# Head-by-head key and query loads with 32 partitions outermost, a later value load, and new durations in a hand-written plan: sketched linear attention and a ReGLU block on Trainium2

## The chip, the cores and the metric

One Trainium2 chip, one core. The metric is the device time of one launch in microseconds (us), the median over runs. All times below are us from the start of the profiled span unless a unit is given. PE is TensorE (matmul), DVE VectorE, ACT ScalarE, POOL GpSimd, SP SyncE; SP, ACT and POOL also issue the transfers (DMAs).

## What is computed

Four batches b, four heads h, 1088 positions, head size 32, sketch rank 8, then a feed-forward block over 4352 tokens of width 128 with 1536 hidden columns:

```
phi(x) = outer(S1 x, S2 x) flattened           # 64 features per position
kv = sum_s phi(k) v^T ;  z = sum_s phi(k)      # per batch and head
attn = (phi(q) kv) / (phi(q) z + 1e-6)
x = attn as [4352, 128]                        # heads side by side
out = (relu(x w_gate) * (x w_val)) w_out
```

q, k, v, the sketches, the weights and the output are float32; the wide matmuls run in float16.

## The kernel before

**Stages.** For each batch a key object K(b) loads the keys, transposes them on DVE (`t1`, or `t1q` for batch 0, and `t1r` for the last 64 positions), sketches them on PE (L330), transposes back (`t2`, L350), sums z on PE (`zsum`, L364), masks it on DVE (`zevac`, L370), multiplies it out on PE (`w`, L377) and writes it into the query weights on ACT (`wevac`, L382); POOL (DVE for one part of batch 0) makes the outer products (`phi`, L249), and PE accumulates kv with the values (L389). The values of batch 0 are loaded as float32 into `v32` and cast on ACT (L307); the others are cast by their DMA. Nine query groups Q(g) (the first with 8 columns of 32 positions per head, the others with 16, so that a group can reach over a batch's edge) go through DVE transpose (L459), sketch on PE (L468), transpose back on DVE (L475), denominator (POOL L485, DVE L489 and L493), outer products (POOL L497, L249), PE transpose (L509), ACT copy (L513), PE product with kv (L521) and ACT copy into `xT` (L528). The feed-forward block is cut into 51 pairs, 3 for group 0 and 6 for each other group: gate and value matmuls (L553), relu on ACT (L566), product on DVE (L570), output matmuls (L579), and at the end of a group a scaled copy on ACT (L585) and stores on SP (L605).

**Order.** Each engine runs its instructions strictly in the order in which they were written. The start is written out by hand: loads of batch 0 on SP and ACT (L164 to L174), then constants, the weight loads on POOL, and 48 idle matmuls on zeros (L222) that keep PE busy before its first real work (L225, L230). Everything after goes into `Plan`, a list scheduler in Python (L21 to L76): each operation is added with an engine, a duration, dependencies, a due time and an earliest time `at`; `Plan.run` simulates the engines and picks by latest start. Only the order comes out of it: nothing waits for a planned time on the chip. The inputs of the plan are the durations in the `P.add` calls, the landing times of the loads (`land`, `qland`, L533 to L538), the time of the first pair `T0` and the step between pairs `PACE` (L255, L256), and the time from which each engine is free (L649). Where the planned gap on PE before the first pair is long, L655 fills in more matmuls on zeros.

**Loads.** Keys go in four blocks of 256 positions for a batch, each for all four heads (L138); the last 64 positions in a load of their own (L143); queries in one load per batch (for batch 0 in two, columns 0 to 8 first, L172 and L174). In `load_k` the outermost dimension of the source is the head:

```
eng.dma_start(out=kA[b][:, blk], in_=k[b, :, 256*blk:256*blk+256, :].rearrange("h (t q) d -> h t (q d)", q=8))
```

The built program gives the loads and stores of SP and ACT together eight completion semaphores in rotation: from the ninth on, each issue waits on its queue until the load issued eight places before has landed. SP issues in this order: S2, blocks 0 and 2 of batch 0, its rest (`load_kr`), the first queries, the rest of the values, the other queries of batch 0, and then for each of the batches 1 to 3 four blocks, the rest and the queries: 25 loads, ahead of the stores. ACT issues S1, blocks 1 and 3, and the values of batch 0, and then loads its function table (L179).

Of the kernel before, what the change touches and what calls it, by code (L numbers as in the profile page):

```python
# [79 lines left out]
def kernel(  # L80
# [12 lines left out]
    nc = tc.nc  # L93

    B, H, S, D = q.shape
    R = S1.shape[0]
# [38 lines left out]
    wv = sb("wv", [DM, NJ, 128], FP16)  # L135
    wo = sb("wo", [128, NJ, DM], FP16)

    def load_k(eng, b, blk):  # L138
        eng.dma_start(out=kA[b][:, blk],
                      in_=k[b, :, 256 * blk:256 * blk + 256, :].rearrange(  # L140
                          "h (t q) d -> h t (q d)", q=8))

    def load_kr(eng, b):  # L143
        eng.dma_start(out=kR[b], in_=k[b, :, 1024:, :].rearrange("h (t e) d -> h t (e d)", e=2))
# [5 lines left out]
    def load_vr(eng, dst, b):  # L150
        eng.dma_start(out=dst[0:64, :, 8, :], in_=v[b, :, 1024:, :].rearrange("h p d -> p h d"))

    def load_q(eng, b, lo, hi):
        eng.dma_start(out=qA[:, b * NT + lo:b * NT + hi, :],
                      in_=q[b].rearrange("h (t n) d -> (h t) n d", n=NT)[:, lo:hi, :])

    def load_w(dst, src, lo, hi):
        nc.gpsimd.dma_start(out=dst[:, lo:hi], in_=src.rearrange("m (j f) -> m j f", f=128)[:, lo:hi])
# [2 lines left out]
        nc.gpsimd.dma_start(  # L161
            out=wo[:, lo:hi], in_=moe_w_out.rearrange("(j f) m -> f j m", f=128)[:, lo:hi])

    nc.scalar.dma_start(out=s16[0:R], in_=S1[:, None, :].to_broadcast([R, 4, D]))  # L164
    nc.sync.dma_start(out=s16[R:2 * R], in_=S2[:, None, :].to_broadcast([R, 4, D]))
    load_k(nc.sync, 0, 0)
    load_k(nc.scalar, 0, 1)
    load_k(nc.sync, 0, 2)
    load_k(nc.scalar, 0, 3)
    load_kr(nc.sync, 0)  # L170
    load_v(nc.scalar, v32, 0)
    load_q(nc.sync, 0, 0, 8)  # L172
    load_vr(nc.sync, v32, 0)
    load_q(nc.sync, 0, 8, NT)  # L174

    zero = sb("zero", [128, 128], FP16)
    nc.vector.memset(zero, 0.0)
    scr = sb("scr", [1, 1], FP16)
    nc.scalar.activation(out=scr, in_=zero[0:1, 0:1], func=ACTF.Relu)  # L179

    id32 = sb("id32", [2 * R, 2 * R])
    make_identity(nc, id32)
# [70 lines left out]
            op=ALU.mult)  # L253

    T0 = 11.5  # L255
    PACE = 1.65  # L256

    class K:


        def __init__(self, b, land, cuts, engs):
            self.b = b
            n, i = f"k{b}", ["DVE", "POOL"]
            self.kT = rot("kT", b, 2, [128, 34, 32])
            self.ab = rot("abk", b, 2, [128, NQ, 2, 2, 2 * R])
            self.kp = rot("kp", b, 2, [128, 2, NQ, 2, R * R], FP16)
            self.zm = rot("zm", b, 2, [128, 4 * R])
            if b == 0:
                t1 = [P.add("DVE", 0.58, lambda x=x: self.t1q(x, x + 4), at=land[0]) for x in (0, 4)]
            else:  # L270
                t1 = [P.add("DVE", 0.6, lambda x=x: self.t1(x, x + 2),
                            [kk[b - 2].kvx] if b > 1 else [], at=land[0]) for x in (0, 2)]
            t1.append(P.add("DVE", 0.14, self.t1r, at=land[-1]))
            ab = []
            for lo, hi in zip(cuts, cuts[1:]):
                ab.append(P.add("PE", 0.09 * (hi - lo), lambda lo=lo, hi=hi: self.sketch(lo, hi),
                                [*t1[:1 if b == 0 and hi == 4 else 3], *ab[-1:]], take=("V", n), lat=0.25))
            t2, ph = [], []
            for lo, hi in zip(cuts, cuts[1:]):
                last = hi == NQ  # L280
                t2.append(P.add("DVE", 0.14 + 0.067 * (hi - lo), lambda lo=lo, hi=hi: self.t2(lo, hi),
                                [ab[len(t2)], *t2[-1:]], give=(n,) if last else ()))
            zs = []
            for lo, hi in zip(cuts, cuts[1:]):
                zs.append(P.add("PE", 0.083 * (hi - lo), lambda lo=lo, hi=hi: self.zsum(lo, hi),
                                [t2[len(zs)], *zs[-1:]], take=("M", n + "m"), lat=0.25))
            self.z = zs[-1]
            zm = P.add("DVE", 0.18, self.zevac, [self.z])
            w = P.add("PE", 0.45, self.w, [zm], lat=0.25)
            self.wst = P.add("ACT", 0.25, self.wevac, [w])  # L290
            kv = []
            for (lo, hi), e in zip(zip(cuts, cuts[1:]), engs):
                for h2 in range(2):
                    eng = e[h2]
                    ph.append(P.add(
                        eng, (0.16 + 0.145 * (hi - lo)) if eng == "DVE" else 0.1 + 0.27 * (hi - lo),
                        lambda h2=h2, lo=lo, hi=hi, eng=eng: self.phi(h2, lo, hi, eng),
                        [t2[cuts.index(lo)]]))
                kv.append(P.add("PE", 0.115 * (hi - lo), lambda lo=lo, hi=hi: self.kv(lo, hi),
                                [self.z, *ph[-2:], *kv[-1:], *self.vdeps(land)], lat=0.25))  # L300
            self.kvx = P.add("DVE", 0.28, self.kvevac, [kv[-1], zm], give=(n + "m",))
# [115 lines left out]
    class Q:  # L417


        def __init__(self, g, land):  # L420
            self.g = g
            n0, nn = self.n0, self.nn = groups[g]
            self.parts = parts(n0, nn)
            bs = [b for b, _, _ in self.parts]
            m = self.m = nn // 2
            self.qT = rot("qT", g, 4, [128, 16, 32])[:, 0:nn]
            self.ab = rot("abq", g, 4, [128, 8, 2, 32])[:, 0:m]
            self.qp = rot("qp", g, 4, [128, 8, 2, R * R], FP16)[:, 0:m]
            self.pt = rot("pt", g, 4, [128, 8, 128], FP16)[:, 0:m]
            self.dn = rot("dn", g, 4, [128, 16])[:, 0:2 * m]  # L430
            self.rd = rot("rd", g, 4, [128, 16])[:, 0:2 * m]
            self.an = rot("an", g, 4, [128, 16, R])[:, 0:2 * m]
            n = f"q{g}"
            f = nn / 16
            need = T0 + PACE * first[g] - 0.2
            old = [qq[g - 4].xx] if g > 3 else []
            t1 = P.add("DVE", 0.06 + 0.52 * f, self.t1, old, at=max(land[b] for b in bs))
            ab = P.add("PE", 0.1 + 0.5 * f, self.sketch, [t1, *(kk[b].wst for b in bs)],
                       take=("V", n), lat=0.25)
            t2 = P.add("DVE", 0.12 + 0.54 * f, self.t2, [ab], give=(n,))  # L440
            e = "DVE" if g == 0 else "POOL"
            d1 = P.add(e, 0.25 if g == 0 else 0.45, lambda: self.bwm(e), [t2])
            d2 = P.add("DVE", 0.15 + 0.15 * f, self.red, [d1])
            d3 = P.add("DVE", 0.2, self.rec, [d2])
            d4 = P.add(e, 0.25 if g == 0 else 0.42, lambda: self.am(e), [d3])
            if g == 0:
                ph = [P.add("DVE", 0.62, lambda: self.phi(0, 3, "DVE"), [d4]),
                      P.add("POOL", 0.42, lambda: self.phi(3, 4, "POOL"), [d4])]
            else:
                ph = [P.add("POOL", 0.08 + 0.235 * 4, lambda lo=lo: self.phi(lo, lo + 4, "POOL"), [d4])  # L450
                      for lo in (0, 4)]
            tr = P.add("PE", 0.47 * f, self.tr, ph, take=("M", n + "t"), lat=0.2)
            te = P.add("ACT", 0.15 + 0.75 * f, self.tre, [tr], give=(n + "t",))
            nu = P.add("PE", 0.2 + 0.25 * f, self.num, [te, *(kk[b].kvx for b in bs)],
                       take=("M", n + "x"), lat=0.25)
            self.xx = P.add("ACT", 0.15 + 0.42 * f, self.x, [nu], give=(n + "x",), due=need - 0.6)

        def t1(self):
            nc.vector.transpose(self.qT.rearrange("p n t -> p (n t)"),  # L459
# [70 lines left out]
                    "p (a t s) -> p a t s", a=4, s=ns),  # L530
                in_=m_ps[:, 0:32 * self.nn].rearrange("p (a s t) -> p a t s", a=4, s=ns))

    kk = [K(0, [4.6, 4.7, 4.9, 5.0, 6.5, 5.2], [0, 4, 9], [("DVE", "POOL"), ("POOL", "POOL")])]  # L533
    qland = [5.5, 14.0, 18.0, 22.0]
    qq = [Q(0, qland)]
    for b in range(1, B):
        kk.append(K(b, [[0, 12.0, 16.0, 20.0][b]] * 2, [0, 5, 9], [("POOL", "POOL")] * 2))
    qland[0] = 8.0  # L538
    for g in range(1, 9):
        qq.append(Q(g, qland))  # L540

# [67 lines left out]
    for i, (g, y) in enumerate(pairs):  # L609
# [3 lines left out]
        for z in range(2):  # L613
            gm.append(P.add("PE", 0.22, lambda i=i, z=z: gate(i, z), [qq[g].xx, lastpe, *gm],
                            due=due + 0.3 * z, take=("G", f"g{i}{z}"), lat=0.2))
            rel.append(P.add("ACT", 0.57, lambda i=i, z=z: relu(i, z),
                             [gm[-1], *(pro[i - 3:i - 2] if i > 2 else [])],
                             due=due + 0.6 + 0.5 * z, give=(f"g{i}{z}",)))
        vm = P.add("PE", 0.435, lambda i=i: val(i), [gm[-1]], due=due + 0.7,
# [12 lines left out]
    for eng, at, fn in [  # L632
# [4 lines left out]
        ("POOL", 9.4, lambda: load_vr(nc.gpsimd, v_sb[1], 1)),  # L637
    ]:
        P.add(eng, 0.6, fn, at=at, due=at + 2.0)
    for b in range(1, B):  # L640
        for blk in range(4):
            P.add("SP", 0.45, lambda b=b, blk=blk: load_k(nc.sync, b, blk), at=5.0, due=4.0 * b)
        P.add("SP", 0.45, lambda b=b: load_kr(nc.sync, b), at=5.0, due=4.0 * b + 0.1)
        P.add("SP", 0.45, lambda b=b: load_q(nc.sync, b, 0, NT), at=5.0, due=4.0 * b + 0.2)
        if b > 1:
            P.add("POOL", 0.8, lambda b=b: load_v(nc.gpsimd, v_sb[b], b), at=6.0 * b, due=8.0 * b)
            P.add("POOL", 0.6, lambda b=b: load_vr(nc.gpsimd, v_sb[b], b), at=6.0 * b, due=8.0 * b)

    order = P.run({"PE": 4.2, "DVE": 4.3, "ACT": 4.2, "POOL": 5.2, "SP": 5.0})  # L649
    pe = 4.2  # L650
    go = qq[0].xx["end"]
    for o in order:
        if o["eng"] == "PE":
# [34 lines left out]
```

## Time and profile before

| what | value |
|---|---|
| runs shown | 136.34, 139.30, 139.46 us, median 139.30 |
| the profiled execution | 136.85 us, of it 135.1 us span |
| PE busy in the span | 112.6 us (83%), 1306 matmuls |
| DVE, ACT, POOL busy | 91.0, 77.0, 51.7 us |
| first transpose of keys (L319) | 13.45 |
| first gate matmul (L553) | 26.28 |
| first product (L570) | 31.22 |
| first gate of group 2, pair 9 of 0 to 50 (L553) | 51.02 |
| last output copy (L585) ends | 128.07 |
| mean granted PE clock | 0.916 |

The page divides the span into 40 slices of 3.38 us. Busy shares and the granted clock are in tenths of each slice. A busy PE is not PE at its peak, since the ends of matmuls are modelled. In the chain of work that ended last each row has a start, a length and the instruction or the transfer that held the end back. In the timeline a row has a start, a length, engine, line, operation, tiles and the count, and in brackets how long the engine had been idle and what ended that.

### The profile page before, as it was taken

The numbers are of one execution on the slowest core, as the hardware profiler recorded it, in microseconds if no ns is written. First come the engines' busy times: TensorE is split into PE (matmuls) and PEld (weight loads), VectorE is DVE, ScalarE is ACT, GpSimd is POOL, SyncE is SP. The second block draws the span as 40 slices with busy tenths as digits, with TensorE's granted clock in tenths as the row PEclk, the third lists the DMA queues.
The fourth block names the chain that finished last, engine by engine and source line by source line (L and its number), as shares of the span: only waits on it lengthen the run. The fifth ranks groups of instructions, "written<-read, shape, count | busy, mean of one in ns | idle before, by whom it ended". The sixth has DMA issues, their size and how long they took to land.

```text
span 135.1 us, 3196 instructions
## 1 busy us (share of the span) xinstructions
PE 112.6 (83%) x1306; PEld 73.5 (54%) x1306; DVE 91.0 (67%) x145; ACT 77.0 (57%) x137; POOL 51.7 (38%) x73
## 2 busy tenths in 40 slices
PE   6930799963989999999999999999999999999500
PEld 6920486842645763747675374766546556546200
DVE  4010678719369989888897885689678799579400
ACT  0400120383255668974876896577599988898300
POOL 7400393992761527109570700946170017000000
PEclk9995555999599999999999999999999999999965
DMA  0699337999635510110020011013002103012011
GB/s 11 146 261 230 82 117 210 156 142 245 104 80 116 180 64 0 22 58 5 13 69 0 2 29 53 0 13 70 0 0 43 39 0 63 17 14 71 0 30 48
DMA packets 10143, 9.47 MB, mean 70 GB/s; under 512 B 3664, under 2 KB 8400, under 8 KB 10128
## 3 DMA queue, kind: packets, MB, share of 16 engines
q1 hardware_dynamic: 4752, 6.46, 17.4%
q0 software_dynamic: 4544, 2.02, 12.3%
q10 hardware_dynamic: 832, 0.79, 1.8%
q8 instruction: 10, 0.16, 0.5%
q14 instruction: 5, 0.04, 0.1%
HBM read 9.05 MB, written 2.23 MB: 83 GB/s over the span
## 4 chain that ended last, share of the span: by engine, by line
PE 51%; DMA 18%; ACT 10%; DVE 4%; issue 4%; POOL 3%; SPq 3%; ACTq 1%; POOLq 1%; DVEq 0%
PE g_ps L553 14%; PE o_ps L579 12%; PE d_ps L553 12%; DMA v<-in_v_dram 10%; DMA kA<-in_k_dram 8%; ACT g_sb L566 4%; ACT pt L513 3%; DVE ht L570 3%; PE m_ps L509 3%; POOL qp L249 2%; PE m_ps L364 2%; PE m_ps L521 2%; PE d_ps L330 2%; PE d_ps L468 2%; ACT xT L528 2%
## 5 line engine op out<-in xcount | busy, mean ns | idle before, releaser
L566 ACT ACTIVATE g_sb<-g_ps 128x512 f16<-128x512 f32 x102 | 56.9, 599 | 19.7 <-PE g_ps L553 18.3
L570 DVE TENSOR_TENSOR ht<-g_sb,d_ps 128x1024 f16<-128x1024 f16 x51 | 61.1, 1209 | 10.1 <-ACT g_sb L566 6.3
L553 PE MATMUL g_ps<-xT,wg 128*128 128x512 f16 (+1 forms) x108 | 35.1, 367 | 1.5 <-ACT g_sb L566 0.3
L579 PEld LDWEIGHTS <-ht 128*128 128x128 f16 x408 | 27.6, 114 | 10.8 <-DVE ht L570 4.0
L579 PE MATMUL o_ps<-wo,ht 128*128 128x128 f16 x408 | 31.8, 221 | 0.7 <-DVE ht L570 0.7
L553 PE MATMUL d_ps<-xT,wv 128*128 128x512 f16 (+1 forms) x108 | 30.8, 372 | 0.0
L249 POOL TENSOR_TENSOR kp<-abk 128x640 f16<-128x640 f32 (+1 forms) x15 | 17.4, 1181 | 28.4 <-DVE abk L350 28.4
L249 POOL TENSOR_TENSOR qp<-an,abq 128x512 f16<-128x512 f32 (+1 forms) x17 | 17.5, 1050 | 3.0 <-DVE an L497 2.4
L553 PEld LDWEIGHTS <-wg 128*128 128x128 f16 x108 | 10.1, 100 | 9.2 <-issue 3.3
L513 ACT COPY pt<-m_ps 128x1024 f16<-128x1024 f16 (+1 forms) x9 | 8.7, 963 | 7.8 <-PE m_ps L509 7.7
L220 PE MATMUL o_ps<-zero 128*128 128x128 f16 x115 | 11.6, 277 | 1.1 <-DVE mask L204 1.1
L485 POOL TENSOR_TENSOR bw<-abq 128x128 f32<-128x128 f32 x8 | 3.6, 456 | 23.0 <-DVE abq L475 23.0
L553 PEld LDWEIGHTS <-wv 128*128 128x128 f16 x108 | 9.2, 98 | 5.9 <-issue 2.6
L330 PE MATMUL d_ps<-kT,skS 64*32 64x160 f32 (+2 forms) x128 | 4.2, 329 | 9.5 <-DVE kT L319 6.4
L220 PEld LDWEIGHTS <-zero 128*128 128x128 f16 x115 | 9.9, 129 | 1.8 <-DVE mask L204 1.1
L475 DVE STREAM_TRANSPOSE abq<-d_ps 128x512 f32<-128x512 f32 (+1 forms) x9 | 6.1, 683 | 2.7 <-PE d_ps L468 2.7
L330 PEld LDWEIGHTS d_ps<-kT,skS 64*32 64x32 f32 x128 | 1.6, 117 | 11.6 <-DVE kT L319 6.6
L311 DVE STREAM_TRANSPOSE kT<-kA 128x512 f32<-128x512 f32 x6 | 4.1, 681 | 5.1 <-DMA kA<-in_k_dram 5.1
L585 ACT ACTIVATE o_sb<-o_ps 128x512 f32<-128x512 f32 (+1 forms) x9 | 5.2, 573 | 2.5 <-PE o_ps L579 2.5
L459 DVE STREAM_TRANSPOSE qT<-qA 128x512 f32<-128x512 f32 (+1 forms) x9 | 5.8, 652 | 1.1 <-DMA qA<-in_q_dram 1.1
L468 PE MATMUL d_ps<-qT,wst 64*64 64x256 f32 (+7 forms) x96 | 6.5, 368 | 0.0
L307 ACT CAST v_sb<-v 128x1152 f16<-128x1152 f32 x1 | 1.2, 1152 | 9.3 <-DMA v<-in_v_dram 9.3
(66 smaller groups left out, 84.0 us busy)
## 6 DMA issues: line engine op xcount, KB each, us to landing
kA<-in_k_dram SPq DMA_DIRECT2D x14, 128.0 KB
qA<-in_q_dram SPq DMA_DIRECT2D x3, 544.0 KB
out_dram<-o_sb SPq DMA_DIRECT2D x5, 256.0 KB
v_sb<-in_v_dram POOLq DMA_DIRECT2D x3, 256.0 KB, 9.2
v<-in_v_dram ACTq DMA_DIRECT2D x1, 512.0 KB
qA<-in_q_dram SPq DMA_DIRECT2D x1, 416.0 KB
out_dram<-o_sb SPq DMA_DIRECT2D x2, 192.0 KB
kA<-in_k_dram ACTq DMA_DIRECT2D x2, 128.0 KB
```

The lines of the kernel that those rows point to most:

```text
L220: nc.tensor.matmul(o_ps[:, 0], zero, zero, start=True, stop=True)
L249: eng.tensor_tensor(out=dst.rearrange("p x (i j) -> p x i j", i=R), in0=a[:, :, :, None].to_broadcast([128, n, R, R]), in1=b[:, :, None, : ...
L330: nc.tensor.matmul(d[32 * blk:32 * blk + 32, hp, 32 * lo:32 * top], skS[r].rearrange("p a f -> p (a f)"), kT[r, 8 * blk + lo:8 * blk + top ...
L459: nc.vector.transpose(self.qT.rearrange("p n t -> p (n t)"), qA[:, self.n0:self.n0 + self.nn].rearrange("p n d -> p (n d)"))
L468: nc.tensor.matmul(d[64 * c:64 * c + 64, hp, 32 * lo:32 * hi], wst[r, b].rearrange("p a f -> p (a f)"), self.qT[r].rearrange("p (n c) t -> ...
L475: nc.vector.transpose(self.ab.rearrange("p n a f -> p a n f"), ps(f"q{self.g}")[:, :, 0:32 * self.m].rearrange("p a (n t) -> p a n t", t=32))
L513: nc.scalar.copy(out=self.pt.rearrange("f n s -> f (n s)"), in_=m_ps.bitcast(FP16)[:, 0:128 * self.m])
L553: nc.tensor.matmul(d[:, (y - lo) * W:(y - lo + 1) * W], w[:, js[y]], xT[:, xs], start=True, stop=True)
L566: nc.scalar.activation(out=g_t[i][:, z], in_=ps1(f"g{i}{z}"), func=ACTF.Relu)
L570: nc.vector.tensor_tensor(out=h_t[i].rearrange("p (a c) -> p a c", a=2), in0=g_t.pop(i), in1=ps(f"v{i}"), op=ALU.mult)
L579: nc.tensor.matmul(o_ps[:, s], ht[:, y * W + s:(y + 1) * W:ns], wo[:, j], start=(j == 0 and s == 0), stop=j == NJ - 1, skip_group_check=True)
L585: nc.scalar.mul(out=o_t[g][:, 0:ns], in_=o_ps[:, 0:ns], mul=1.0 / (XSCALE * XSCALE))
```

## The change

Key loads and query loads go head by head, with 32 partitions as the outermost dimension of source and destination. The first queries of batch 0 are one load for all heads. The sketches S1 and S2 are issued behind the keys, and the values of batch 0 behind ACT's first activation. The other queries of batch 0 move from the hand-written start into the plan. In the plan, durations, landing times, PACE and the engines' start times are replaced. The arithmetic and the tiles stay.

```
-    def load_k(eng, b, blk):
-        eng.dma_start(out=kA[b][:, blk],
-                      in_=k[b, :, 256 * blk:256 * blk + 256, :].rearrange(
-                          "h (t q) d -> h t (q d)", q=8))
+    def load_k(eng, b, h):
+        eng.dma_start(out=kA[b][32 * h:32 * h + 32].rearrange("t b q d -> t b (q d)"),
+                      in_=k[b, h, 0:1024, :].rearrange("(b t q) d -> t b (q d)", b=4, q=8))
...
-    def load_q(eng, b, lo, hi):
-        eng.dma_start(out=qA[:, b * NT + lo:b * NT + hi, :],
-                      in_=q[b].rearrange("h (t n) d -> (h t) n d", n=NT)[:, lo:hi, :])
+    def load_q(eng, b, h, lo, hi):
+        eng.dma_start(out=qA[32 * h:32 * h + 32, b * NT + lo:b * NT + hi, :],
+                      in_=q[b, h].rearrange("(t n) d -> t n d", n=NT)[:, lo:hi, :])
...
-    nc.scalar.dma_start(out=s16[0:R], in_=S1[:, None, :].to_broadcast([R, 4, D]))
-    nc.sync.dma_start(out=s16[R:2 * R], in_=S2[:, None, :].to_broadcast([R, 4, D]))
     load_k(nc.sync, 0, 0)
     load_k(nc.scalar, 0, 1)
     load_k(nc.sync, 0, 2)
     load_k(nc.scalar, 0, 3)
+    nc.scalar.dma_start(out=s16[0:R], in_=S1[:, None, :].to_broadcast([R, 4, D]))
+    nc.sync.dma_start(out=s16[R:2 * R], in_=S2[:, None, :].to_broadcast([R, 4, D]))
     load_kr(nc.sync, 0)
-    load_v(nc.scalar, v32, 0)
-    load_q(nc.sync, 0, 0, 8)
+    nc.sync.dma_start(out=qA[:, 0:8, :],
+                      in_=q[0].rearrange("h (t n) d -> h t n d", n=NT)[:, :, 0:8, :].rearrange(
+                          "h t n d -> h t (n d)"))
     load_vr(nc.sync, v32, 0)
-    load_q(nc.sync, 0, 8, NT)
...
     nc.scalar.activation(out=scr, in_=zero[0:1, 0:1], func=ACTF.Relu)
+    load_v(nc.scalar, v32, 0)
...
-    PACE = 1.65
+    PACE = 1.5
...
-    kk = [K(0, [4.6, 4.7, 4.9, 5.0, 6.5, 5.2], [0, 4, 9], [("DVE", "POOL"), ("POOL", "POOL")])]
-    qland = [5.5, 14.0, 18.0, 22.0]
+    kk = [K(0, [4.8, 4.8, 4.8, 4.8, 7.2, 5.3], [0, 4, 9], [("DVE", "POOL"), ("POOL", "POOL")])]
+    qland = [6.3, 16.0, 20.0, 24.0]
...
-        kk.append(K(b, [[0, 12.0, 16.0, 20.0][b]] * 2, [0, 5, 9], [("POOL", "POOL")] * 2))
-    qland[0] = 8.0
+        kk.append(K(b, [[0, 14.0, 18.0, 22.0][b]] * 2, [0, 5, 9], [("POOL", "POOL")] * 2))
+    qland[0] = 9.0
...
-    for b in range(1, B):
-        for blk in range(4):
-            P.add("SP", 0.45, lambda b=b, blk=blk: load_k(nc.sync, b, blk), at=5.0, due=4.0 * b)
-        P.add("SP", 0.45, lambda b=b: load_kr(nc.sync, b), at=5.0, due=4.0 * b + 0.1)
-        P.add("SP", 0.45, lambda b=b: load_q(nc.sync, b, 0, NT), at=5.0, due=4.0 * b + 0.2)
+    for b in range(B):
+        if b:
+            for h in range(H):
+                P.add("SP", 0.55, lambda b=b, h=h: load_k(nc.sync, b, h), at=5.0, due=4.0 * b)
+            P.add("SP", 0.6, lambda b=b: load_kr(nc.sync, b), at=5.0, due=4.0 * b + 0.1)
+        for h in range(H):
+            P.add("SP", 0.6, lambda b=b, h=h: load_q(nc.sync, b, h, 0 if b else 8, NT), at=5.0,
+                  due=4.0 * b + 0.2)
...
-    order = P.run({"PE": 4.2, "DVE": 4.3, "ACT": 4.2, "POOL": 5.2, "SP": 5.0})
-    pe = 4.2
+    order = P.run({"PE": 5.0, "DVE": 4.3, "ACT": 5.2, "POOL": 5.2, "SP": 6.0})
+    pe = 5.0
```

The other edits are durations of the plan: for instance the key outer products on POOL from 0.1 + 0.27 n to 0.13 + 0.226 n, on DVE from 0.16 + 0.145 n to 0.05 + 0.43 n, relu from 0.57 to 0.53, the ACT copies of a full query group from 0.90 and 0.57 to 1.00 and 0.61. In the built program SP then has 37 loads ahead of the stores (two key heads, S2, the rest of the keys, first queries, rest of the values, four query heads, and for each other batch four key heads, the rest, four query heads); the number of matmuls on zeros goes from 115 to 118; and on DVE, the transposes of the keys of batch 2 now stand behind the eighth product, where their first half stood ahead of the first, while the key transposes of batch 1 and the query transposes of groups 2 and 3, which need the queries of batch 1, stand ahead of the first product in both.

## The prediction

> **What bounds the kernel now.** I read the slices of the page first, then the stretches, the timeline of the first 36 us, the chain, and last the page's DMA queues.
>
> ```profile
> PEclk9995555999599999999999999999999999999965
> DMA  0699337999635510110020011013002103012011
> ...
> q10 hardware_dynamic: 832, 0.79, 1.8%
> ```
>
> ```profile
> 3.00:6.00 3.00, 3.00 (x31) 3.00 (x30) 0.20 (x3) 1.49 (x2) 1.95 (x5) 1.00 0.52 112
> 9.00:12.00 3.00, 0.00 (x0) 0.00 (x0) 0.00 (x0) 0.00 (x0) 0.00 (x0) 0.67 1.36 274
> 26.00:31.00 5.00, 3.34 (x32) 2.28 (x29) 1.95 (x5) 3.87 (x7) 4.91 (x7) 1.00 1.03 167
> 31.00:37.00 6.00, 4.54 (x82) 3.12 (x83) 3.92 (x6) 1.20 (x3) 2.66 (x3) 0.74 0.98 167
> 37.00:51.00 14.00, 13.13 (x156) 8.40 (x155) 12.06 (x18) 8.70 (x16) 5.93 (x8) 0.99 0.38 107
> 51.00:102.00 51.00, 49.38 (x595) 30.49 (x595) 41.28 (x55) 38.36 (x70) 23.64 (x28) 1.00 0.10 22
> ```
>
> A stretch has its length, then the busy time of PE, PEld, DVE, ACT and POOL, the granted PE clock, the DMA share and GB/s. From 51 to 102 PE is busy for 49.38 of 51 us at full clock and the DMAs are nearly idle: PE bounds that part, and no load can shorten it. From 9 to 12 no engine works at all. The clock is at half from 10.0 to 23.7 and from 33.9 to 37.3. All that the change can win lies before 51 us.
>
> ```profile
> 13.45 1.30 DVE L319 STREAM_TRANSPOSE kT<-kA 128x512 f32<-128x512 f32 x2 [6.07 <-DMA qA<-in_q_dram]
> 16.48 1.15 ACT L307 CAST v_sb<-v 128x1152 f16<-128x1152 f32 x1 [9.34 <-DMA v<-in_v_dram]
> 20.02 0.70 DVE L459 STREAM_TRANSPOSE qT<-qA 128x512 f32<-128x512 f32 x1
> 22.93 1.69 PE L220 MATMUL o_ps<-zero 128*128 128x128 f16 x21
> 24.46 0.39 PE L509 MATMUL m_ps<-ident,qp 128*128 128x128 f16 x4
> 26.28 0.60 PE L553 MATMUL g_ps<-xT,wg 128*128 128x256 f16 x4
> 30.59 0.71 DVE L311 STREAM_TRANSPOSE kT<-kA 128x512 f32<-128x512 f32 x1 [3.05 <-DMA kA<-in_k_dram]
> ```
>
> ```profile
> 2.89 13.34 DMA v<-in_v_dram
> ...
> 16.24 0.52 SPq L139
> ...
> 19.95 10.55 DMA kA<-in_k_dram
> ...
> 31.22 1.19 DVE ht L570
> ```
>
> DVE had the sketches ready at 7.38 and then waited for the keys until 13.45. The releaser named is the query load, but the completion counts in the trace put the four key blocks of batch 0 at 5.4, 6.9, 11.9 and 13.25. The second wait is at 30.59: the first half of the keys of batch 2 stands ahead of the first product, and holds DVE for 3.05 us. In the chain both the value load and the eight-semaphore rotation (an SP issue that waits for the values) carry the way there.
>
> Why the keys are slow is in queue 10, which is ACT's: 832 packets are 32 (S1) + 2 x 128 (two key blocks) + 512 (values) = 800 of data and 32 completions. 8 + 4 + 4 + 16 gives 32: a load runs on as many DMA engines as its outermost dimension allows, S1 on 8, the values on 16, a key block on 4. The counts agree: of the first queries' 16 completions 12 came by 10.2 and four by 15.7; of the values' 12 by 11.4 and four by 16.2. Four engines carry all the keys and delay whatever is spread over all 16.
>
> **Part by part.**
>
> *Keys of batch 0.* With 32 outermost a head runs on 16 engines. Today's first key packet follows its issue (1.26) by 1.4 us; after, the first issue is at 0.81, so packets from 2.2. 524 KB at 274 GB/s take 1.9 us, at 112 GB/s (the lowest rate of a stretch with traffic of this kind) 4.7: landed between 4.1 and 6.9. Both lie before 7.38, where DVE has finished S1bd behind the 48 zero matmuls, so the wait of 6.07 goes whole. Then the sketches' S1 and S2, moved behind four issues (0.64 and 0.73 each), are late next: packets at about 3.6, and PE needs them at 6.29; cover 2 us or more, and if it fails each late us costs one.
>
> A rule speaks against the head by head form. The Trainium skill, SBUF — State Buffer, section Door 1, says that 32 partitions reach only 8 of the 16 write ports, and that 0 to 63 reach no more. By it (an estimate from its 27.2 GB/s a port) the heads, two at a time on the same eight ports, would take 2.4 us together instead of 1.2. No row of this case shows a load of 32 partitions over 16 engines; by the page the keys land 1.2 us later, and the time is the same, since the cover ends at 7.38.
>
> *Values.* They are issued after two key issues, S1, the table load (1.28) and its activation (0.20): 0.81 + 1.37 + 0.60 + 1.48 and gaps, so 4.4 instead of 2.89. Lower bound of landing 11.4 (what lies before them in the DMAs is the same), upper 16.2 + 1.5 = 17.7; I take 12.9, the 12 unburdened completions (11.4) and the later issue. Cast until 14.15 (1.15). Behind the cast on ACT stands wevac, which without it would run at 7.4 + 6.18 = 13.6 (19.63 - 13.45 today); it runs at 14.2: 0.6 lost, from -0.6 to 5 by the bounds.
>
> *To the first gate.* Today 26.28 - 13.45 = 12.83 from the first key transpose. In the new order DVE makes the transpose of group 1 (0.70) after L485 instead of while it waited for PE, and PE's sketch of group 1 follows it, then 22 zero matmuls, then L509. Sketch end 7.4 + 10.2 to 10.7, zeros 1.2 us at full clock or 1.8 at half (today's 21 took 1.69): L509 at 7.4 + 11.3 to 12.4 (the 0.6 included), today 10.95 after. So the first gate is at 7.4 + 12.83 + 0.35 to 1.45 = 20.6 to 21.7; I take 21.1, as the clock is unknown. 5.2 us won.
>
> *To the first product.* DVE, from its own rows: outer product of group 0 ends at 7.4 + 10.85; POOL's next value issue (0.81) and L485 (0.47) end at 12.4; reduce and reciprocal to 13.0; then two key transposes (1.38), the rest (0.20), two query transposes (1.3): first product at 7.4 + 15.95 = 23.35, today 31.22. 7.9 won, since the half of batch 2 is no longer ahead.
>
> What must have landed: keys of batch 1 by 20.4, queries of batch 1 by 22.0. SP's issue of the fourth key head waits, by the rotation, for the values (12.9). Then come it, the rest and four query heads, six issues of 0.64: last issued at 16.8. The shortest landing of a key load today is 4.1 us (1.26 to 5.4), the longest 10.3 (issued 8.85, landed 19.13). So 20.9 to 27. I take 20.9, because the loads have no four busy engines any more; the cover is then 1.1 us, the thinnest of all.
>
> *To pair 9.* Here the chain is PE. From L509 of group 1 (POOL's outer products end at 23.0; PE at 23.45) to the first gate of pair 9 the new order has 8 gate and value pairs of 0.86, 7 outputs of 0.45, keys 0.39 + 0.79 + 0.36 + 1.0, queries 0.35 + 0.60 + 0.45 + 0.35 + 0.60, in full-clock times of 49 to 68 us: 14.9 us. At the busy share of 37 to 51 (13.13 of 14) 15.9: pair 9 at 39.4. Today it is at 51.02; there half a clock and the batch-2 wait cost. 11.6 won, less two outputs (0.9) that the new order has not done by then: 10.7.
>
> *The rest* holds the same matmuls; the lead of preparations changes a little with PACE. No row prices that; the bounds are PE's lost 1.6 us of 51 to 102 as gain, and as loss twice that. I take 0. 12 more issues on SP end far ahead of the first store. Three more zero matmuls cost 0.2 us at most, counted above.
>
> **Sum.** The profiled execution took 136.85 us (135.1 of span); 136.85 - 10.7 = 126.15, say 126.2. It stands 2.45 below the median of the runs shown (139.3), so a median after may be that much higher too.
>
> **Rivals.**
>
> A. *The first product waits for the queries of batch 1.* DVE is in order, and their transposes stand ahead of all products. For it: SP's issue is tied to the values, and the cover is 1.1 us. With a landing at 7 us (between 4.1 and 10.3) they are there at 23.8, at 10.3 at 27.1: then the first product is at 25 to 28.5, 3 to 6 us won, and with the later half clock gone 1.7 more. About 131, from 129 to 133.5.
>
> B. *The change does not do what it says:* the keys are held by volume, not by four engines, and land at 11 to 13 as now. For it: 9 to 12 us shows a DMA share of 1.36 and 274 GB/s. Against: 12 of 16 completions come 5 us before the other four. Only the batch-2 wait goes: 136.85 - 3.05, about 134 to 137.
>
> C. *Slower: eight small loads in flight.* The rotation allows eight loads, now of 128 KB and 104 to 136 KB where there were 544 KB. If each takes d to land, the queries of batch 1, at places 19 to 22, are there at 0.8 + (22/8 + 1) d. The first product comes no earlier than now if that is over 29.9, so from d = 7.8 us; at the 9 us of the slower blocks they land at 34.6, the first product is at 36, and the time 4.8 more: 141. For it: blocks of today took 5.9 to 10.3. Against: those sat on four engines.
>
> **How the numbers follow.** Forecast 62 in 100 (its own range 123.5 to 129, from the values at 11.4 to 14, the clock, and the rest); better than 123.5: 4; A 18; B 9; C 7. The measurement tells about 2% from no change, so faster is below 134.1: forecast, better, A, and a part of B, 0.84 in all; same 0.09; slower 0.07. To leave out no more than 2 in 10 the range goes from 122 to 132.5, through most of A.
>
> **What would show it.** First key transpose at 7.4, not 13.45; ACT's cast at 13; wevac at 14.2; first gate near 21; no DMA wait on DVE ahead of the first product, which is near 23.4; pair 9 near 39.4; the same 86 us from there to the end, within 1.5. If DVE idles on qA before the first product it is A; if key completions still come in two batches it is B; if SP's issues stretch to over 1 us each throughout, C. I am wrong if the clock drops anew between 20 and 40 us, or if the new order leaves PE idle after pair 9.

## The result, and the profile after

The changed kernel takes 123.92 us (median of four runs, 123.37 to 124.77). The kernel before took 138.25 us beside it (136.34 to 139.46). Two of the four runs before (139.3 and 139.46) were in a slower state that some executions fall into, and all ratios here leave such runs out. The ratio is 0.907, with a 95% interval from 0.896 to 0.917: faster, and inside the range given. The profiled execution took 123.37 us, 121.6 of it span; predicted were 126.2.

First the same slices of the page as before (here of 3.04 us each), and queue 10.

```profile
PEclk9999558999999999999999999999999999999995
DMA  3999999999810021002001100040011021012021
...
q10 hardware_dynamic: 856, 0.79, 2.2%
```

The DMAs are busy from 3 us to 30 us without the holes of before; the half clock fills two slices and a part of the next (12.5 to 19.4) instead of five, and does not come back before the last slice. Queue 10 has 856 packets: the same 800 of data, and 56 completions instead of 32, which are 8 for S1, 16 for each of the two key heads and 16 for the values. So each of ACT's two key loads now runs on 16 engines.

Then the stretches after, in the columns explained in the prediction, and the timeline.

```profile
6.00:9.00 3.00, 2.02 (x50) 1.31 (x55) 2.17 (x6) 0.30 (x1) 0.23 (x1) 1.00 1.12 270
9.00:12.00 3.00, 2.77 (x70) 2.23 (x50) 2.13 (x4) 0.29 (x1) 2.81 (x3) 1.00 1.42 250
24.00:27.00 3.00, 3.00 (x41) 2.02 (x40) 2.14 (x4) 2.22 (x5) 2.69 (x3) 1.00 1.34 203
31.00:37.00 6.00, 5.94 (x73) 3.72 (x71) 5.65 (x9) 4.77 (x10) 2.57 (x4) 1.00 0.37 91
51.00:102.00 51.00, 50.00 (x573) 30.66 (x571) 43.54 (x55) 39.40 (x71) 19.36 (x24) 1.00 0.12 27
```

```profile
3.35 0.40 ACTq L146 DMA_DIRECT2D v<-in_v_dram  x1
...
6.91 1.30 DVE L319 STREAM_TRANSPOSE kT<-kA 128x512 f32<-128x512 f32 x2
...
11.71 1.15 ACT L307 CAST v_sb<-v 128x1152 f16<-128x1152 f32 x1 [4.87 <-DMA v<-in_v_dram]
...
12.77 0.18 ACT L382 ACTIVATE wst<-m_ps 128x16 f32<-128x16 f32 x1
...
13.00 0.70 PE L468 MATMUL d_ps<-qT,wst 64*64 64x128 f32 x8 [1.22 <-ACT wst L382]
...
16.30 2.53 PE L220 MATMUL o_ps<-zero 128*128 128x128 f16 x22
...
18.62 0.63 PE L509 MATMUL m_ps<-ident,qp 128*128 128x128 f16 x4
...
20.69 0.60 PE L553 MATMUL g_ps<-xT,wg 128*128 128x256 f16 x4
...
21.14 1.31 DVE L459 STREAM_TRANSPOSE qT<-qA 128x512 f32<-128x512 f32 x2 [1.30 <-DMA qA<-in_q_dram]
22.37 1.18 DVE L570 TENSOR_TENSOR ht<-g_sb,d_ps 128x1024 f16<-128x1024 f16 x1
```

From 9 to 12 us, where nothing worked before, PE is busy for 2.77 of 3 us at full clock. The transpose at 6.91 has no bracket: no wait for the keys is left there (by the completion counts the four heads landed at 3.33, 3.67, 4.53 and 4.76, where the blocks took until 13.25). At 13.00 PE had waited 1.22 us for ACT, which had first to cast the values; at 21.14 DVE had waited 1.30 us for the queries of batch 1. These two waits are what is left of the old ones.

The milestones of every run's profiled execution, in us. "First product to pair 9" and "pair 9 to end" (end of the last output copy) are differences of the rows.

| kernel | first key transpose | write into query weights (L382) | first gate | first product | first product to pair 9 | pair 9 to end | median us |
|---|---|---|---|---|---|---|---|
| before | 13.45 | 19.63 | 26.28 | 31.22 | 19.80 | 77.05 | 138.25 |
| after | 6.91 | 12.77 | 20.69 | 22.37 | 15.86 | 76.52 | 123.92 |
| e1 key form only | 7.34 | 15.08 | 22.32 | 24.78 | 17.34 | 77.04 | 128.93 |
| e2 after, old key form | 14.13 | 20.43 | 26.99 | 29.27 | 15.86 | 76.52 | 131.11 |
| e3 after, old plan | 7.14 | 15.05 | 21.89 | 24.07 | 17.34 | 77.04 | 127.69 |
| e4 before, new plan | 13.79 | 20.40 | 26.93 | 28.77 | 16.11 | 76.52 | 129.90 |
| e5 after, PACE 1.65 | 6.68 | 14.01 | 21.03 | 22.81 | 19.01 | 76.55 | 126.27 |
| e6 after, old plan but PACE | 6.96 | 14.23 | 21.12 | 22.66 | 15.74 | 77.13 | 123.92 |
| e7 after, values earlier | 7.17 | 15.07 | 22.46 | 23.99 | 15.90 | 76.52 | 124.94 |
| e8 after, heads exchanged | 6.42 | 14.43 | 21.19 | 23.51 | 15.86 | 76.51 | 124.62 |
| e9 after, whole query loads | 7.21 | 14.30 | 21.95 | 23.48 | 15.90 | 76.50 | 124.31 |
| e10 after, few zeros | 6.88 | 13.64 | 20.38 | 23.12 | 15.86 | 76.53 | 124.28 |
| e11 after, first product free | 6.13 | 11.07 | 19.34 | 20.87 | 16.08 | 76.16 | 121.79 |
| e13 e7, rest by head | 6.92 | 15.38 | 22.34 | 23.87 | 16.03 | 76.52 | 125.30 |

### The profile page after: what moved, and what is told of

Its sections match the earlier page's. It is cut to its first block, busy times and chain, and to the rows that moved or that the text cites. A ratio compares the mean times of both kernels' runs of the same rounds, so it can differ in the third digit from the quotient of the medians.

```text
span 121.6 us, 3222 instructions
## 1 busy us (share of the span) xinstructions
PE 108.7 (89%) x1309; PEld 70.7 (58%) x1309; DVE 90.0 (74%) x145; ACT 75.4 (62%) x137; POOL 52.1 (43%) x73
## 5 line engine op out<-in xcount | busy, mean ns | idle before, releaser
L566 ACT ACTIVATE g_sb<-g_ps 128x512 f16<-128x512 f32 x102 | 56.1, 598 | 14.8 <-PE g_ps L553 13.7
L579 PEld LDWEIGHTS <-ht 128*128 128x128 f16 x408 | 26.8, 113 | 11.5 <-DVE ht L570 3.0
L553 PE MATMUL g_ps<-xT,wg 128*128 128x512 f16 (+1 forms) x108 | 33.2, 368 | 0.2
L553 PEld LDWEIGHTS <-wv 128*128 128x128 f16 x108 | 9.8, 99 | 8.5 <-issue 1.9
L220 PEld LDWEIGHTS <-zero 128*128 128x128 f16 x118 | 10.3, 130 | 2.7 <-issue 1.3
L553 PEld LDWEIGHTS <-wg 128*128 128x128 f16 x108 | 8.6, 98 | 4.5 <-issue 1.8
L497 POOL TENSOR_TENSOR an<-abq,rd 128x128 f32<-128x128 f32 x8 | 3.3, 406 | 14.8 <-DVE rd L493 9.3
L509 PE MATMUL m_ps<-ident,qp 128*128 128x128 f16 x68 | 5.5, 224 | 0.7 <-DVE kv_bd L396 0.6
L509 PEld LDWEIGHTS <-qp 128*128 128x128 f16 x68 | 4.5, 101 | 2.4 <-issue 1.8
L528 ACT CAST xT<-m_ps 128x512 f16<-128x512 f32 (+1 forms) x9 | 5.2, 578 | 0.4 <-PE m_ps L521 0.4
```

The lines of the kernel that those rows point to most:

```text
L220: nc.tensor.matmul(o_ps[:, 0], zero, zero, start=True, stop=True)
L509: nc.tensor.transpose(t[:, 128 * i:128 * i + 128], self.qp[:, i].rearrange("p a f -> p (a f)"), ident)
L528: nc.scalar.copy(out=xT[:, 32 * self.n0:32 * (self.n0 + self.nn)].rearrange("p (a t s) -> p a t s", a=4, s=ns), in_=m_ps[:, 0:32 * self.nn ...
L553: nc.tensor.matmul(d[:, (y - lo) * W:(y - lo + 1) * W], w[:, js[y]], xT[:, xs], start=True, stop=True)
L566: nc.scalar.activation(out=g_t[i][:, z], in_=ps1(f"g{i}{z}"), func=ACTF.Relu)
L579: nc.tensor.matmul(o_ps[:, s], ht[:, y * W + s:(y + 1) * W:ns], wo[:, j], start=(j == 0 and s == 0), stop=j == NJ - 1, skip_group_check=True)
```

## Experiments

**e1, the form of the key loads alone.** The kernel before with nothing but the new `load_k` and its calls.

```
-        eng.dma_start(out=kA[b][:, blk],
-                      in_=k[b, :, 256 * blk:256 * blk + 256, :].rearrange("h (t q) d -> h t (q d)", q=8))
+        eng.dma_start(out=kA[b][32 * h:32 * h + 32].rearrange("t b q d -> t b (q d)"),
+                      in_=k[b, h, 0:1024, :].rearrange("(b t q) d -> t b (q d)", b=4, q=8))
```

> The kernel before with nothing changed but load_k: keys head by head, 32 partitions outermost. Theory T (four DMA engines carried all the keys): first key transpose near 7.4 instead of 13.45, first gate near 20.2, the hold on the keys of batch 2 ahead of the first product mostly gone since they too land sooner; 123 to 128 us. Rival V (the order of the loads and the later values bring the gain, not the engines): first key transpose at 11 or later, 134 us or more. Rival P (the new plan brings the gain after the first gate): first gate near 20.2 but the time no better than 130.

Measured: 128.93 us (127.96 to 129.06), ratio 0.937 (0.929 to 0.945). Two waits of DVE in its timeline tell why it stopped short of the forecast:

```profile
10.31 0.25 DVE L314 STREAM_TRANSPOSE kT<-kR 128x64 f32<-128x64 f32 x1 [1.68 <-DMA kR<-in_k_dram]
...
24.14 0.71 DVE L310 STREAM_TRANSPOSE kT<-kA 128x512 f32<-128x512 f32 x1 [1.16 <-DMA kA<-in_k_dram]
```

The four key blocks are indeed cured by their form. But the load of the last 64 positions, behind them, kept its four engines and now ends last (at 10.29), and the half of batch 2's keys ahead of the first product still costs 1.16 us. The forecast did not have the first, and the second only as mostly gone.

**e2, all of the change but the form of the key loads.** The old `load_k` in the changed kernel.

```
-        eng.dma_start(out=kA[b][32 * h:32 * h + 32].rearrange("t b q d -> t b (q d)"),
...
+        eng.dma_start(out=kA[b][:, blk],
...
```

> The changed kernel with the old load_k alone, keys in four blocks over all heads. T: the keys land at 11.5 to 13 again, first gate near 25.5, no hold of batch 2 ahead of the first product, 131 to 135 us. V: first key transpose at 9 or earlier, 126 us or less.

Measured: 131.11 us (130.4 to 132.15), ratio 0.955 (0.946 to 0.965). As expected in size; the timeline of PE adds something:

```profile
12.94 0.25 PE L226 MATMUL m_ps<-id,s 16*128 16x16 f32 x1 [6.58 <-DMA s<-in_S_dram]
```

The first key transpose (14.13) is held not by keys, which were all there at 12.56, but by the sketches, which now stand behind the blocks and landed at 12.85. Issuing S1 and S2 last is safe only because the keys ahead of them are quick: after, they landed at 5.20.

**e3 and e4, loads and plan apart.** e3 is the changed kernel with every number of the plan as before (durations, landings, PACE, engine starts); the diff shows two of them. e4 is the kernel before with those numbers new.

```
-    PACE = 1.5
+    PACE = 1.65
...
-    qland = [6.3, 16.0, 20.0, 24.0]
+    qland = [5.5, 14.0, 18.0, 22.0]
...
```

> The changed kernel with all durations, landing times, PACE and start times of the plan as before; the loads stay changed. T: first key transpose at 6.9, first gate 20 to 21; the old order puts half of batch 2's keys ahead of the first product, but they land by about 24: 124 to 126.5 us. P: 128 us or more.

> The kernel before with the new numbers of the plan alone; loads as before. T: first key transpose still at 13.4, first gate near 26.5, first product held by the queries of batch 1 that land at 26: near 28.5, so 132 to 135 us. P: 128 us or less.

Measured: e3 127.69 us (127.11 to 129.43), ratio 0.928 (0.920 to 0.937); e4 129.90 us (129.81 to 130.16), ratio 0.946 (0.939 to 0.953). Both lie between the two theories. In e4, where the keys still come late, DVE shows the old wait; in e3 (the second view) most of the wait for batch 2's keys is gone:

```profile
13.79 1.30 DVE L319 STREAM_TRANSPOSE kT<-kA 128x512 f32<-128x512 f32 x2 [6.53 <-DMA kA<-in_k_dram]
```

```profile
23.43 0.71 DVE L311 STREAM_TRANSPOSE kT<-kA 128x512 f32<-128x512 f32 x1 [0.78 <-DMA kA<-in_k_dram]
```

By the ratios, new loads alone take 7.2% off, the new plan alone 5.4%, both 9.3%. The sum of the two is 3.3 points, some 4.5 us, more than both together, because each removes the same stall by itself: DVE held by the half of batch 2's keys ahead of the first product. It was 3.05 us before; in e3, where quick loads make these keys earlier, it is 0.78 us, and in e4, where the new order needs them later, it is gone. The half clock of before from 33.9 to 37.3, which follows that stall, is in neither of the two. What the theory of e4 left out: the new order also makes the way from the first product to pair 9 shorter (16.11 for 19.80).

**e5 and e6, which number of the plan.** e5 is the changed kernel with PACE alone put back (the diff); e6 has all other numbers put back and PACE kept.

```
-    PACE = 1.5
+    PACE = 1.65
```

> The changed kernel with PACE back at 1.65, nothing else. Measured so far, from the first gate of pair 9 to the last output copy: 77.05 us with the old plan, 76.52 with the new one, and from the first product to pair 9's gate 17.3 (old plan, new loads) and 15.9 (new plan). Theory PACE (the step between pairs sets the order and so both gains): these go back to about 77.0 and 17.3, and the time is near 126. Theory durations (the new durations set them): they stay at 76.5 and 15.9, 124 us.

> The changed kernel with all numbers of the plan as before except PACE, which stays at 1.5. Theory PACE: 76.5 from pair 9's gate to the end and 15.9 before it, 124 to 125 us. Theory durations: 77.0 and 17.3, 126 us or more.

Measured: e5 126.27 us (125.9 to 126.83), ratio 0.921 (0.916 to 0.926); e6 123.92 us (123.33 to 124.17), ratio 0.902 (0.896 to 0.907). PACE is worth 2.3 us by e5 (and 3.8 with the other numbers of before, e3 against e6); the measured durations and landings together nothing that the median shows. DVE's timeline and a stretch of e5 show what PACE does:

```profile
22.81 1.18 DVE L570 TENSOR_TENSOR ht<-g_sb,d_ps 128x1024 f16<-128x1024 f16 x1
25.87 0.71 DVE L311 STREAM_TRANSPOSE kT<-kA 128x512 f32<-128x512 f32 x1 [1.88 <-DMA kA<-in_k_dram]
26.51 0.47 DVE L350 STREAM_TRANSPOSE abk<-d_ps 128x320 f32<-128x320 f32 x1
26.90 1.18 DVE L570 TENSOR_TENSOR ht<-g_sb,d_ps 128x1024 f16<-128x1024 f16 x1
```

```profile
24.00:27.00 3.00, 1.16 (x22) 0.40 (x22) 1.13 (x3) 2.02 (x5) 0.92 (x2) 1.00 1.26 212
```

With 1.65 the planner puts the first half of batch 2's keys ahead of the second product; they have not landed (their last head came at 25.68), the product behind them waits, and PE is busy for 1.16 of 3 us, where after it is busy for all three. The durations give 0.5 us from pair 9 to the end (76.2 to 76.6 in the runs with the new ones, whatever the PACE, 77.0 to 77.1 in those with the old); in e6 the median shows no loss by it.

**e7, values earlier.** `load_v` ahead of ACT's first activation.

```
+    load_v(nc.scalar, v32, 0)
     zero = sb("zero", [128, 128], FP16)
...
-    load_v(nc.scalar, v32, 0)
```

> The changed kernel with the value load of batch 0 ahead of the table load again. If the wait for the values behind which the query weights are written (1.22 us on PE ahead of the first query sketch) is worth what it shows: cast near 10.9 instead of 11.7, first gate 0.5 to 0.9 earlier, and the time 0 to 0.6 less. Rival: the earlier values delay the first queries or the keys on the same DMA engines and nothing is gained.

Measured: 124.94 us (123.74 to 126.23), ratio 0.909 (0.904 to 0.914). The large load of the values was there at 10.30, earlier than in any run that has the key heads and issues it behind the activation (11.63 to 13.91). But the cast needs the rest of the values too, the small load of SP (`load_vr`); that came at 11.84, so the cast was no earlier (11.86). And the rest of the keys was late:

```profile
10.20 0.25 DVE L315 STREAM_TRANSPOSE kT<-kR 128x64 f32<-128x64 f32 x1 [1.74 <-DMA kR<-in_k_dram]
```

The first gate is 1.8 us later in its execution, the median 1.0 more, though the runs overlap. This is the rival of the expectation: the rest of the keys landed at 10.18 here and 10.29 in e1, where the values are issued at 2.35 and 2.25, and between 7.0 and 9.3 in the changed kernel and the seven runs that issue the values behind the activation and load the key heads as it does.

**e13, that rest head by head too.** e7, with batch 0's rest as four loads of 32 outermost.

```
-        eng.dma_start(out=kR[b], in_=k[b, :, 1024:, :].rearrange("h (t e) d -> h t (e d)", e=2))
+        for h in range(H):
+            eng.dma_start(out=kR[b][32*h:32*h+32], in_=k[b, h, 1024:, :].rearrange("(t e) d -> t e d", e=2))
```

> The kernel with the early value load (124.94 us, where DVE waited 1.74 us for the rest of batch 0's keys at 10.20) with that rest, too, loaded head by head, 32 partitions outermost, in four loads instead of one. Nothing else differs from it. Theory: that load ran on four engines behind the values, as the key blocks of the kernel before did; on 16 it lands by 8.0, DVE's wait is gone, the second stage is at 13.0 to 13.5 instead of 15.07 (the write into the query weights), the first gate at 20.5 to 21.2 instead of 22.46, and the time 123.2 to 124.0. Rival: it is the volume ahead of it, or the three further issues on SP (0.6 us each), that make it late: it lands at 9.5 or later, first gate 22 or later, 124.5 to 125.5.

Measured: 125.30 us (125.02 to 125.82), ratio 0.916 (0.907 to 0.925). The theory fell. The timeline of DVE, and a row of SP's waits (line waited for, sum, times, longest):

```profile
10.50 0.24 DVE L319 STREAM_TRANSPOSE kT<-kR 128x64 f32<-128x64 f32 x1 [2.28 <-DMA kR<-in_k_dram]
```

```profile
SPq L144 <- DMA kA<-in_k_dram: 2.0, 2, 1.9
```

The four small loads ran on 16 engines (16 completions each), the first landed at 5.9, but two had to wait by the rotation for key heads before they could be issued. SP was done with issuing the last at 5.72, behind the issue of the values (2.35), and it landed at 10.31. The three later ones all came behind the values' last completion (8.36). Sixteen engines are not enough by themselves: the place behind other loads counts too.

**e10, fewer zeros.** Six matmuls on zeros instead of 22 ahead of the first L509.

```
-                warm(n)
+                warm(n if n < 20 else 6)
```

> The changed kernel with 6 instead of 22 matmuls on zeros ahead of the first transposes of the query products. The 22 run from 16.30 to 18.83 and the transposes wait behind them to 18.62, though the outer products end at 16.61. If the zeros only cost time there: first gate 1.2 to 1.8 earlier, but the first product is held by the queries of batch 1 at 21.1, so 0.3 to 1.2 us less in all. Rival: without them the clock stays at half longer, the first gate moves less than 1 us and the time is the same or longer.

Measured: 124.28 us (123.35 to 124.44), ratio 0.905 (0.901 to 0.909): no change. The first gate is 0.3 earlier, although the values came 0.9 later in this execution (cast at 12.58 instead of 11.71). From the cast to the first gate it takes 7.80 us instead of 8.98; but e8, with all the zeros, takes 7.81, so what they cost is not shown. And the first product is held by the queries of batch 1 (DVE waited 1.19 for them, until 21.89).

**e8, key heads exchanged between the queues.**

```
-    load_k(nc.scalar, 0, 1)
-    load_k(nc.sync, 0, 2)
+    load_k(nc.scalar, 0, 2)
+    load_k(nc.sync, 0, 1)
```

> The changed kernel with heads 1 and 2 of batch 0's keys exchanged between the queues: heads 0 and 1 on SP, 2 and 3 on ACT, so that the two loads in flight together are heads 0 and 2, then 1 and 3. In the changed kernel heads 0 and 1 landed at 3.33 and 3.67 us and heads 2 and 3 at 4.52 and 4.76. Theory 1: each pair was held by the place in SBUF that it shares (the first pair's 262 KB need 1.4 us from the first packet at about 2.2). Then the pairs, now spread over both halves of the partitions, land about 0.5 us earlier, the last head by 4.2, with neither half of a pair behind the other. Theory 2: the issues and the engines set the pace, and the place does not count: landings within 0.2 us of 3.5 and 4.7. By both the first key transpose stays at 6.9 to 7.2, where DVE waits for the sketches, and the time stays within 1 us of 123.9. The Trainium skill, SBUF - State Buffer, section Door 1, is for theory 1: the first 64 partitions reach only half of the write ports.

Measured: the heads landed at 3.47, 3.73, 4.15 and 4.33; time 124.62 us (124.49 to 124.94), ratio 0.911 (0.906 to 0.915), unchanged within the scatter. The last head came 0.4 us before that of the changed kernel, and 0.45 to 1.0 before those of e7, e9, e11 and e13, which keep its arrangement (4.78 to 5.35). The first pair came no earlier (3.73 against 3.67 to 4.32 in the five). And counted from the first completion of any head (2.75 here, 3.15 after), the four took 1.58 us here and 1.61 in the changed kernel. So the theory of the place is not shown by this one execution. The Trainium skill, SBUF — State Buffer, section Door 1, says that partitions 0 to 63 reach one half of the write ports and 64 to 127 the other; the last landing agrees in direction, but no run here shows that it set the pace.

**e9, queries of a batch in one load of 128 partitions.**

```
-        for h in range(H): load_q(nc.sync, b, h, 0 if b else 8, NT)
+        load_qb(nc.sync, b, 0 if b else 8, NT)
```

> The changed kernel with the queries in one load for all heads (128 partitions) instead of four: for the rest of batch 0 and for batches 1 to 3. The queries of batch 1 are then load 17 and not 20 to 23, six issues of SP (0.5 to 0.6 us each) fewer ahead of their last packet. In the changed kernel they landed at 21.1, and DVE idled 1.30 us for them ahead of the first product. Theory: the many issues and the rotation of eight are what makes them late. Then they land by 19.5, DVE does not wait, the first product is at 21.3 to 21.8 instead of 22.37, and the time is 123.0 to 123.6. Rival: one load of 544 KB takes the longer for its size, or the volume ahead sets the landing: at 20.5 or later, first product and time as in the changed kernel, 123.6 to 124.5.

Measured: 124.31 us (122.56 to 124.67), ratio 0.901 (0.875 to 0.928): inconclusive on the time. The queries of batch 1 landed at 19.15, as the theory had it, and DVE's wait for them is gone:

```profile
21.25 1.26 DVE L463 STREAM_TRANSPOSE qT<-qA 128x512 f32<-128x512 f32 x2
23.48 1.22 DVE L574 TENSOR_TENSOR ht<-g_sb,d_ps 128x1024 f16<-128x1024 f16 x1 [0.97 <-ACT g_sb L570]
```

But in this execution, the slowest of the four, the values landed at 13.2 (11.6 after), the write into the query weights was 1.5 us later, and the first product waited for the gate. In e8, e10 and e11, whose loads up to there are issued as after (but for the exchange in e8), the cast began at 13.38, 12.58 and 13.12, so such a spread comes without this edit. Whether the earlier issue of batch 1's keys delays the values here stays open.

**e11, three things off the way to the first product.** The plan is told later landings, so that ACT's write into the query weights stands ahead of the cast, and the query transposes of groups 2 and 3 behind the first product; at most 8 zeros fill a gap.

```
-    kk = [K(0, [4.8, 4.8, 4.8, 4.8, 7.2, 5.3], ...
-    qland = [6.3, 16.0, 20.0, 24.0]
+    kk = [K(0, [4.8, 4.8, 4.8, 4.8, 9.6, 5.3], ...
+    qland = [6.3, 19.0, 23.0, 27.0]
...
-                warm(int((o["start"] - pe - 0.15) * 0.8 / 0.056))
+                warm(min(8, int((o["start"] - pe - 0.15) * 0.8 / 0.056)))
```

> The changed kernel with three inputs of the plan moved towards what the trace showed: values at 9.6 (ACT's write into the query weights then stands ahead of the cast), queries of batches 1 to 3 at 19, 23 and 27 (the transposes of groups 2 and 3 then stand behind the first product), and at most 8 matmuls on zeros in a gap. Theory: the cast (0.6 us), the zeros (0.3 us in the run with six) and the wait for the queries of batch 1 (1.2 to 1.3 us) each hold the first products: together first gate at 19.8 to 20.2, first product at 20.8 to 21.4, pair 9 at 36.8 to 37.5, time 122.5 to 123.3. Rival: DVE pays for the moved transposes between the first product and pair 9, or the clock stays at half longer without the zeros: pair 9 at 38 or later and the time 123.5 to 125.

Measured: 121.79 us (120.91 to 122.2), ratio 0.889 (0.880 to 0.898). Every run is below every run of the changed kernel, and the time is better than both theory and rival had it. Its timeline:

```profile
11.07 0.18 ACT L382 ACTIVATE wst<-m_ps 128x16 f32<-128x16 f32 x1 [5.02 <-PE m_ps L377]
...
13.12 1.15 ACT L307 CAST v_sb<-v 128x1152 f16<-128x1152 f32 x1 [1.86 <-DMA v<-in_v_dram]
...
20.87 1.22 DVE L570 TENSOR_TENSOR ht<-g_sb,d_ps 128x1024 f16<-128x1024 f16 x1 [1.07 <-ACT g_sb L566]
...
23.33 0.67 DVE L459 STREAM_TRANSPOSE qT<-qA 128x512 f32<-128x512 f32 x1
```

The values landed late here too, at 13.0, and it no longer matters for the write, which now waits only for PE. The moved transposes cost little behind it: 16.08 instead of 15.86 us to pair 9. It is 2.1 us better, more than expected; in the profiled execution the half clock lasted 3.4 us instead of 6.8. Of the 1.35 us by which the first gate is earlier there, 0.78 is the first key transpose (6.13 for 6.91), which none of the three edits touches; the last section says what moves it. How the gain divides among the three edits was not tried; fewer zeros alone gave nothing in the time (e10).

## Why the prediction was right, step by step

The gain was 13.5 us in the profiled executions (136.85 to 123.37) where 10.7 were forecast. The mechanism was the one forecast, key heads on 16 engines and batch 2's keys behind the first products, but some steps came out by errors that cancel.

- *Keys of batch 0* (first transpose 7.4, not 13.45): 6.91, and 4.76 for the last head, inside 4.1 to 6.9. e1 and e2 show that the form of the load does it.
- *The sketches next* (cover of 2 us): they cost nothing after, but they landed at 5.20 and PE took them at 6.04, so the cover was 0.8 us. e2 shows the price when it is gone.
- *Values* (12.9; write at 14.2): 11.6 and 12.77. The step took the issue at 4.4, behind the table load. It was at 3.35, while the table load ran (2.40 to 3.68), and what it waited for was the rotation: the values are the ninth load and reuse the semaphore of the first key head, which landed at 3.33. In the seven other runs with these loads of keys and values the issue follows that landing by 0.02 to 0.03 us too (3.40 to 3.78), and in e2 it follows block 0 (6.58, issue at 6.60). The step missed this wait. The landings of those runs, 11.6 to 13.9, hold the predicted value, and the changed kernel's is the earliest of them, so that part is luck. That the cast stands ahead of the write was right, and e11 shows its worth.
- *First gate* (21.1): 20.69. From the first key transpose 13.78 us, inside the 13.18 to 14.28 worked out. L509 came 11.71 after it, inside its bounds too, by two errors: the sketch of group 1 ended 9.5 us after the first key transpose, not 10.2 to 10.7, and the 22 zeros took 2.53 us, not 1.2 to 1.8. The 1.8 was read from 21 zeros that ran at half clock only until 23.7.
- *First product* (23.35): 22.37. The thin cover of 1.1 us was indeed gone: the queries of batch 1, put at 20.9, landed at 21.02 and released DVE at 21.14. That the time fits is luck: SP issued the last of them at 15.2, not 16.8, and it took 5.8 us to land, not 4.1. (The longest landing quoted, 10.3 us, is misread as well: the block that landed at 19.13 was issued at 7.45.) Rival A happened in small: DVE idled 1.30 us, but the product was 1 us ahead of the forecast. The part with batch 2's keys was right as an effect; that PACE alone does it (e5, e6) was not in the prediction, which read the built order and not the edit behind it.
- *To pair 9* (39.4): 38.23, 15.86 after the first product where 16.05 were worked out. The clock did not drop anew.
- *Less two outputs* (0.9) and *the rest* (0): this step was mis-sized. Sixteen output matmuls fewer were done by pair 9 (56 for 72), as said, yet the way from there to the end became 0.53 us shorter. The two stretches, before and after:

```profile
51.02:128.07 77.05, 73.52 (x816) 44.77 (x815) 61.45 (x73) 59.38 (x106) 26.58 (x32) 1.00 0.11 26
```

```profile
38.23:114.75 76.52, 73.85 (x836) 44.73 (x832) 63.70 (x78) 58.54 (x106) 26.90 (x32) 1.00 0.11 26
```

PE's busy time rose by 0.33 and its idle time fell from 3.53 to 2.67. e5 separates the two causes. It has the new durations, and 72 output matmuls done by pair 9 as before, and its stretch takes 76.55 us: so deferring sixteen more costs nothing, and the 0.5 us are the new durations (e3, with the old ones and 72: 77.04). How PE takes sixteen more matmuls in the same time is not shown; its busy time in e5 is 73.81, against 73.85.
- *Sum*: pair 9 came 1.17 earlier than forecast, the 0.9 was not due, and the rest, with the launch, gave 0.7: 2.8 us, the whole of 126.15 less 123.37.

Rival B (held by volume) is out for the key heads: their completions come 16 at a time, by 4.76. Rival C (eight small loads) shows only faintly: SP waited 3.5 us in the rotation for the rest of the values, and the queries of batch 1 were there at 21.02, not at 34.6.

## What to carry to other kernels

Count the completions of a load against its data packets: here a load on 4 of 16 engines delayed itself and the last four completions of whatever was spread over all 16, by some 5 us. Read in the built order which transfer stands ahead of the first real work of an in-order engine; a planner's step (here PACE) can put one there, while its durations could be wrong with little harm (0.5 us). When two edits remove the same stall, test each alone and both: their gains do not add.

## What the runs showed that was not expected

In the profiled executions the half clock between 9 and 25 us comes in steps: it lasted 3.4 us in e5 and e11, 6.8 after and in e6, e8, e10, 10.2 in e1, e3, e7, e9 and e13, and 13.7 before and in e2 and e4. What adds or saves a step is not shown. It is not the kernel alone, since the four runs of the changed kernel had mean clocks from 0.941 to 0.964, and 3.4 us at half clock are 0.014 of its span. The Trainium skill, TensorE: Matmul & The Clock Gate, section Part 1, names a free-running window of about 3.4 us; the steps agree with it.

The profile shows full clock from the start of the span, but the 48 matmuls on zeros there say otherwise: they follow each other every 106 ns until the profile's first record of the full clock and every 56 ns from it on (107 ns in the later half clock). That record comes at 3.75 us in e11, 4.69 in e8, 5.71 after and 6.70 in e1, and the first key transpose, which stands behind these matmuls, comes in the same order: 6.13, 6.42, 6.91 and 7.34. So up to 1.2 us of the differences between rows of the table of milestones are not the edits'.

The landing of the values scatters by 2.3 us between the changed kernel, e3, e5, e6, e8, e10 and e11, which issue the loads up to there alike but for the exchange in e8 (cast at 11.71 to 13.99). In e8 twelve of its 16 completions had come at 11.2 and the last four followed until 13.3, so a few engines set the end even of a load that is spread over all.
